# Value weights transposed by DMA on the way in, and newly searched instruction orders, in a recurrent-memory transformer on one core

## The chip, the cores and the metric

The kernel runs on one core of one Trainium2 chip. A core has a matrix engine (TensorE, "PE" in the profile, with its weight loads as "PEld"), three engines for elementwise work (VectorE "DVE", ScalarE "ACT", GpSimd "POOL"), a queue engine (SyncE, "SP") and 16 DMA engines. The metric is the device time of one execution in microseconds (us); less is better. Kernels are compared by the median of their runs.

## What is computed

Two rounds of a recurrent-memory attention layer and a gated MLP, each behind a layer norm and with a residual, on 2048 tokens of width 448:

```python
def _A_ref(x, mem0, Wq, Wk, Wv, Wo, seg_len):      # 16 heads of 256, 8 memory rows, segments of 32
    ...
    for s in range(n_seg):                          # 64 segments, one after the other
        xs = x[:, s * seg_len:(s + 1) * seg_len, :].copy()
        h = jnp.concatenate([mem, xs], axis=1)
        q = jnp.einsum('btd,dhe->bhte', h, Wq)
        k = jnp.einsum('btd,dhe->bhte', h, Wk)
        v = jnp.einsum('btd,dhe->bhte', h, Wv)
        scores = jnp.einsum('bhqe,bhke->bhqk', q, k) * scale
        scores = jnp.where(mask[None, None], scores, -1000000000.0)
        p = _softmax(scores, axis=-1)
        o = jnp.einsum('bhqk,bhke->bhqe', p, v)
        o = jnp.einsum('bhte,hed->btd', o, Wo)
        mem = o[:, :M, :].copy()
        outs.append(o[:, M:, :])
    return jnp.concatenate(outs, axis=1)

def _B_ref(x, W_gate, W_up, W_down):
    gate = jnp.einsum('bsd,df->bsf', x, W_gate)
    up = jnp.einsum('bsd,df->bsf', x, W_up)
    gate = gate * (lambda x, dt: x.astype(dt))(gate > 0, gate.dtype)
    h = gate * up
    return jnp.einsum('bsf,fd->bsd', h, W_down)

x = x + _A_ref(_layernorm(x, axis=-1), A_mem0, A_Wq, A_Wk, A_Wv, A_Wo, A_seg_len)
x = x + _B_ref(_layernorm(x, axis=-1), B_W_gate, B_W_up, B_W_down)
```

The last two lines run twice, with the same weights. All tensors are bf16. The memory rows of a segment come out of the segment before it, so each attention layer is a chain of 64 steps.

## The kernel before

**Folded weights.** Queries and keys are never formed. Per head the kernel builds A = Wq Wk^T (448 x 448) and B = Wv Wo (448 x 448) once and works with these: scores are h A h^T, and the output is the sum over heads of (p h) B. `weights()` does this in the start-up. A product over the head's 256 dims needs that dim on the partitions. Wo lies so in DRAM; Wq, Wk and Wv have their 448 input dims first, so they are loaded as they are into staging slots (`Wst`) and transposed.

For Wv this runs per pair of heads, `p` = 0 to 7. `load` (line 1146) brings 384 of the 448 rows of the pair's 512 columns into slot `sv`; two small DMAs (line 1149) bring the other 64 rows, the "tail"; one DMA (line 1150) brings the pair's Wo into `Wos[so]`. `transposes` (lines 1071 to 1093) makes, per head, seven 128 x 128 transposes on PE into one PSUM bank (six on line 1084, one on line 1085) and two evictions on ACT or DVE into `WT` (lines 1088 and 1091, recorded under the helper's lines 273 and 276). `product` (lines 1095 to 1106) then makes two matmuls of 448 columns (line 1102) from `WT` and `Wos`, and one eviction into `Bsb`: three products per head and one for both tails. The five Wv slots lie in `glu` (12 to 14), where the MLP weights go later, and in `Ug` (15, 16); the profile shows these names. Pairs 5 to 7 use slots 12 to 14 again.

**The two layers run side by side.** `chain` does one step of the recurrence for the first layer and, seven segments behind, one for the second, in the same matmuls: the state's products with A (line 1270), their turn and the scores (1427, 1450), a softmax, the weighted rows (1514, 1518), the product with B (1307), sums on DVE (1324) and the new memory (1349). Around it stands the work that no chain waits for: per tile of 128 tokens the attention of the tokens (`att_group`, lines 1603, 1632, 1514, 1670), norms, and the MLP (`glu_units` line 1692, `glu_down` line 1710).

**Small transposes by DMA.** `turn_dma` (lines 1043 and 1044) issues a transposing DMA on SP. It is used from SBUF to SBUF for the probabilities of the tiles (`Tx<-Px`, 96 times), for the MLP's input (`G<-xn`, 64) and for the probabilities of ridden-along tokens (`PTr<-Pr`, 62).

**A written order.** `_Sched.add` collects 9235 operations with what they read and write. What runs where and when is not left to rules: `ORDER` lists all operations once, each entry being five times the operation's index plus the number of its engine (PE, ACT, DVE, POOL, SP). Each engine runs its own operations in that order and waits at semaphores for what the others must have done. `BANKS` gives the PSUM bank of each allocation in the same order. `FILLS` puts idle matmuls on PE ahead of a given entry: position to (how many, bank, mode); each is a 128 x 128 matmul of a zero tile (line 178). These three tables come from a search outside the kernel.

**DMA semaphores.** DMA n uses semaphore n mod `N_DMA`, and `add` (lines 118 to 123) makes it depend on DMA n - `N_DMA`, which used the semaphore before it. At the end SP waits for the last `N_DMA` entries of its queue that are DMAs (lines 240 to 244).

Of the kernel before, what the change touches and what calls it, by code (L numbers as in the profile page):

```python
# [11 lines left out]
D = 448  # L12
# [38 lines left out]
class _Sched:  # L51
# [5 lines left out]
    N_DMA = 48  # L57
# [222 lines left out]
def bass_interleave_layers__memory_aug_recurrent_mem_tr__glu_gated_reglu__prompt_kernel(  # L280
# [536 lines left out]
class _Kernel:  # L817
# [233 lines left out]
    def weights(self):  # L1051
# [91 lines left out]
        for p in range(NPAIR):  # L1143
# [3 lines left out]
            for hh in range(2):  # L1147
                c = 512 * p + 256 * hh
                self.dma(self.Wst[sv][64 * hh:64 * hh + 64, 3, 0:256], self.Wv_d[0:64, c:c + 256], 32768, w=[("Wt", sv, hh)])
# [688 lines left out]
```

## Time and profile before

| | |
|---|---|
| median of 3 runs | 1563.47 us (1560.84 to 1564.4) |
| the profiled execution | 1558.09 us, of which its span is 1556.3 us |
| granted PE clock | 0.998 |
| instructions | 84947 |
| matmuls | 38530 |
| DMA, mean over the span | 32 GB/s; 16.31 MB of the 49.84 MB move in the first 80 us |
| DMA by SP's queue | 44.15 MB in 113168 packets |

The profile is of one execution. Engine times are busy times; matmuls overlap in the array, so that the durations of PE's instructions add up to more than the time that they take, and a group's price is read from the starts of what follows. "Idle before" is put down to what released the engine last. SP's rows show the issue of a DMA; its landing shows as the end of somebody's wait. The program splits into the start-up until about 75 us, in which all weights are loaded and folded, the two chains with the tiles around them, and an end of some 55 us.

### The profile page before, as it was taken

To read this page: it belongs to the slowest core of one execution; us is meant where nothing else is said; L and a number is where in the kernel's file an instruction comes from. 1 tells how busy PE (TensorE), PEld (TensorE's weight loads), DVE (VectorE), ACT (ScalarE), POOL (GpSimd) and SP (SyncE) were. 2 spreads that over 40 slices of the span, in tenths; PEclk is the share of its full clock that TensorE was granted. 3 is DMA by queue.
4 is the path that set the end of the run, shared out by engine and by line. 5 is a ranking of instruction groups with operands and counts; after the bars stand their busy time and mean duration, and the time that the engine had idled before them with its cause. 6 is when DMAs were issued, how large, how long until landed. Compare 5 with 4: busy or idle time off the path is not lost.

```text
span 1556.3 us, 84947 instructions
## 1 busy us (share of the span) xinstructions
PE 1508.1 (97%) x38530; PEld 1097.1 (70%) x38530; DVE 1127.3 (72%) x3284; ACT 820.6 (53%) x2297; POOL 58.0 (4%) x241
## 2 busy tenths in 40 slices
PE   8999999999999999999999999999999999999998
PEld 6676766667667677767767676777768676777766
DVE  8755678677876777778776778677776777767764
ACT  6754556455555545445555555555555556544442
POOL 1000000000000000000000000000000000000000
PEclk9999999999999999999999999999999999999999
DMA  9422000100100100101001101001001111010101
GB/s 266 145 81 56 12 22 16 18 17 17 23 16 19 27 18 20 19 21 24 19 20 21 29 13 28 17 20 25 20 18 19 26 17 28 19 18 21 20 18 27
DMA packets 114167, 49.84 MB, mean 32 GB/s; under 512 B 82824, under 2 KB 113808, under 8 KB 113808
## 3 DMA queue, kind: packets, MB, share of 16 engines
q1 hardware_dynamic: 113168, 44.15, 12.5%
q8 instruction: 304, 4.98, 1.3%
q14 instruction: 55, 0.45, 0.1%
q10 hardware_dynamic: 640, 0.26, 0.1%
HBM read 21.35 MB, written 1.84 MB: 15 GB/s over the span
## 4 chain that ended last, share of the span: by engine, by line
PE 85%; DVE 7%; DMA 5%; ACT 1%; issue 1%; SPq 1%; ACTq 0%; DVEq 0%; POOL 0%
PE psG L1670 14%; PE psG L1603 14%; PE psG L1692 11%; PE psC L1307 11%; PE psC L1270 7%; PE psG L1710 5%; PE psG L1270 3%; PE psG L1514 3%; PE psG L1102 2%; PE psG L1632 2%; PE psC L1427 2%; DMA Tx<-Px 2%; PE psC L1450 1%; PE psC L1514 1%; PE psG L1427 1%
## 5 line engine op out<-in xcount | busy, mean ns | idle before, releaser
L1670 PE MATMUL psG<-Bsb,YT 128*128 128x448 bf16 x1288 | 277.3, 353 | 0.0
L273 ACT ACTIVATE Ug<-psG 64x128 bf16<-64x128 f32 (+2 forms) x441 | 156.7, 370 | 88.9 <-PE psG L1603 72.2
L1692 PE MATMUL psG<-G,glu 64*128 64x128 bf16 x5838 | 184.6, 216 | 11.5 <-DMA G<-xn 5.0
L1307 PE MATMUL psC<-Bsb,YTm 128*32 128x448 bf16 (+2 forms) x4144 | 187.6, 333 | 0.9 <-issue 0.5
L1692 PEld LDWEIGHTS psG<-G,glu 64*128 64x128 bf16 x5838 | 172.6, 94 | 22.0 <-issue 7.9
L1603 PE MATMUL psG<-HT,A 64*128 64x128 bf16 x3332 | 175.7, 217 | 0.3 <-ACT Bsb L273 0.3
L1670 PEld LDWEIGHTS psG<-Bsb,YT 128*128 128x128 bf16 x1288 | 111.1, 97 | 91.2 <-issue 9.5
L1270 PE MATMUL psG<-A,mT 64*32 64x448 bf16 x4424 | 173.7, 350 | 0.3 <-issue 0.3
L1270 PE MATMUL psC<-A,mT 64*32 64x448 bf16 x3416 | 152.8, 350 | 1.9 <-DVE Tr L1476 1.0
L1603 PE MATMUL psG<-HX,A 64*128 64x128 bf16 x2499 | 150.1, 217 | 0.0
L1307 PEld LDWEIGHTS psC<-Bsb,YTm 128*32 128x32 bf16 x4144 | 102.5, 97 | 65.2 <-DVE YTm L276 2.3
L276 DVE CAST Ug<-psG 64x128 bf16<-64x128 f32 (+2 forms) x265 | 111.1, 429 | 23.1 <-PE psG L1603 18.9
L1697 ACT ACTIVATE hG<-psG 128x512 bf16<-128x512 f32 (+1 forms) x125 | 67.9, 543 | 105.3 <-PE psG L1692 99.1
L1603 PEld LDWEIGHTS psG<-HT,A 64*128 64x128 bf16 x3332 | 116.9, 95 | 8.9 <-issue 5.3
L1324 DVE TENSOR_TENSOR Osum<-psC,Osum 32x448 f32<-32x448 f32 (+2 forms) x120 | 73.2, 610 | 68.7 <-ACT Osum L1322 65.9
L276 DVE CAST YT<-psG 128x448 bf16<-128x448 f32 x148 | 90.2, 618 | 41.3 <-PE psG L1518 40.2
L273 ACT ACTIVATE YT<-psG 128x448 bf16<-128x448 f32 x214 | 107.7, 540 | 20.5 <-PE psG L1518 18.2
L1270 PEld LDWEIGHTS psC<-A,mT 64*32 64x32 bf16 x3416 | 76.5, 92 | 53.8 <-ACT mT L273 3.0
L1270 PEld LDWEIGHTS psG<-A,mT 64*32 64x32 bf16 x4424 | 90.3, 92 | 22.0 <-ACT mT L273 1.9
L1710 PE MATMUL psG<-glu,hG 128*128 128x448 bf16 x434 | 97.5, 353 | 0.2 <-DVE hG L1698 0.2
L1698 DVE TENSOR_TENSOR hG<-hG,psG 128x512 bf16<-128x512 bf16 (+1 forms) x113 | 68.9, 617 | 39.3 <-ACT hG L1697 38.4
L1603 PE MATMUL psG<-l,A 64*128 64x128 bf16 x2919 | 97.2, 216 | 0.0
(294 smaller groups left out, 2910.8 us busy)
## 6 DMA issues: line engine op xcount, KB each, us to landing
Bsb<-in_A_Wq_dram SPq DMA_DIRECT2D x6, 384.0 KB
Bsb<-in_A_Wk_dram SPq DMA_DIRECT2D x6, 384.0 KB
glu<-in_A_Wv_dram SPq DMA_DIRECT2D x6, 384.0 KB
Tsb<-Ohi SPq DMA_DIRECT2D x128, 7.0 KB
X<-in_A_x_dram SPq DMA_DIRECT2D x16, 112.0 KB
glu<-in_A_Wo_dram SPq DMA_DIRECT2D x4, 448.0 KB
out_dram<-X SPq DMA_DIRECT2D x16, 112.0 KB
glu<-in_B_W_gate_dram SPq DMA_DIRECT2D x14, 112.0 KB
```

The costliest lines, as they stand in the source:

```text
L273: return E.activation(out, i, ACT.Copy, scale=1.0 if scale is None else scale)
L276: return E.tensor_copy(out, i)
L1270: i = E.matmul(ub[v].ap()[32 * j:32 * j + 32, 0:D], lhsT=self.mT[rw, b, :], rhs=self.A[rw, b, a0:a0 + D], start=(b == 0), stop=(b == 6), t ...
L1307: x = E.matmul(bo.ap()[32 * j:32 * j + 32, 0:d1 - d0], lhsT=self.YTm[:, q, :], rhs=self.Bsb[:, chunks[q], d0:d1], start=(i == 0), stop=(i ...
L1324: s.add("dve", dv_cost(n), lambda E, e, j=j, a_=a_, part=part: E.tensor_tensor(a_, part(j), a_, ALU.add), r=[bo], w=w, part=(j, 0), **P)
L1514: return E.matmul(ps[:, n * q:n * q + n], lhsT=HR[rows, KM + 128 * q:KM + 128 * q + 128], rhs=PT, start=True, stop=True, tile_position=(b, 0))
L1603: i = E.matmul(ub[v].ap()[:, 128 * n:128 * n + 128], lhsT=self.A[rw, b, a0:a0 + 128], rhs=HT[rw, b, :, 0:SEG] if b < 4 else HX[rw, b - 4, ...
L1670: i = E.matmul(bo.ap()[:, 0:D], lhsT=YT[:, c, :], rhs=self.Bsb[:, 14 * g + c, :], start=(g == 0 and c == 0), stop=(g == 3 and c == 13))
L1692: i_ = E.matmul(two[v].ap()[:, 128 * c:128 * c + 128], lhsT=self.Wgu[rw, b, f0:f0 + 128], rhs=G[rw, b, :], start=(b == 0), stop=(b == 6), ...
L1697: s.add("act", 169 + 0.84 * N, lambda E, e, dst=dst, z=two[0], N=N: E.activation(dst, z.ap()[:, 0:N], ACT.Relu), r=[two[0]], w=[("hG", i, ...
L1698: s.add("dve", dv_cost(N), lambda E, e, z=two[1], N=N, dst=dst: E.tensor_tensor(dst, dst, z.ap()[:, 0:N], ALU.mult), r=[two[1]], w=[("hG", ...
L1710: i_ = E.matmul(bk.ap()[:, 0:D], lhsT=hG[:, c, :], rhs=self.Wd[:, c, :], start=(c == 0), stop=(c == NFC - 1))
```

## The change

Three things.

Wv's loads: instead of a plain load of 384 rows, two tail loads and seven PE transposes per head with two evictions, one transposing DMA per pair brings Wv's 448 x 512 block from DRAM straight into the slot, with the head dims on the partitions (`V`). The products read `V` in the slot in place of `WT`. There are 64 operations less. The transfer's size enters the planner's books as 458,752 bytes.

The tables: `ORDER`, `BANKS` and `FILLS` are new from end to end. 44 filling matmuls in four places become 95 in six. In `ORDER`, the first products of the first Wv pair now come ahead of the last transposes of Wq and Wk.

The semaphores: 96 in place of 48.

```diff
-    N_DMA = 48
+    N_DMA = 96
...
 ORDER = (
     206, 2, 8, 199, 211, 204, 22, 142, 138, 12, 226, 219, 148, 231, 224, 246, 239, 153, 17, 251, 58, 244, 27, 32,
...
-FILLS = {1969: (12, 2, 0), 9083: (15, 0, 0), 9211: (7, 0, 0), 9217: (10, 0, 0)}
+FILLS = {54: (8, 1, 0), 67: (35, 1, 0), 76: (7, 1, 0), 1913: (15, 1, 0), 6778: (15, 2, 0), 8162: (15, 1, 0)}
...
         for p in range(NPAIR):
             sv = 12 + p % 5
             so = p % 5
-            load(self.Wv_d, p, sv)
-            for hh in range(2):
-                c = 512 * p + 256 * hh
-                self.dma(self.Wst[sv][64 * hh:64 * hh + 64, 3, 0:256], self.Wv_d[0:64, c:c + 256], 32768, w=[("Wt", sv, hh)])
+            V = self.Wst[sv].rearrange("p a b -> p (a b)")[:, 0:4 * D].rearrange("p (a b) -> p a b", a=4)
+            self.turn_dma(V, self.Wv_d[:, 512 * p:512 * p + 512], 458752, w=[(z, sv) for z in ("Wst", "Wst3")])
             self.dma(self.Wos[so][:, :, :], self.Wo_d[:, 4 * p:4 * p + 4, :], 458752, w=[("Wos", so)])
-            tv = nw()
-            transposes([(sv, hh) for hh in range(2)], tv, True, self.Wst[sv][:, 3, 0:256], [("Wt", sv, hh) for hh in range(2)])
             tails = []
             for hh in range(2):
-                r = tkeys(tv + hh) + [("Wos", so)]
-                rhs = self.Wos[so][:, 2 * hh:2 * hh + 2, :]
+                r = [("Wst", sv), ("Wos", so)]
+                lhs, rhs = V[:, 2 * hh:2 * hh + 2, :], self.Wos[so][:, 2 * hh:2 * hh + 2, :]
                 for k in range(3):
-                    product(self.Bsb[:, b_idx(k, p, hh), :], [(self.WT[tv + hh], 64 + 128 * k, 128, rhs, 0, r)], [("B", p, hh, k)], 0)
-                tails.append((self.WT[tv + hh], 0, 64, rhs, 64 * hh, r))
+                    product(self.Bsb[:, b_idx(k, p, hh), :], [(lhs, 64 + 128 * k, 128, rhs, 0, r)], [("B", p, hh, k)], 0)
+                tails.append((lhs, 0, 64, rhs, 64 * hh, r))
             product(self.Bsb[:, b_tail(p), :], tails, [("B", p, hh, 3) for hh in range(2)], 3)
```

900 rows, old and new, of tables (BANKS, ORDER) are left out of this document.

## The prediction

> **What bounds the kernel now.** I read the busy shares first, then the same by stage, then what TensorE (PE) waited for, then the start-up instruction by instruction.
>
> ```profile
> PE 1508.1 (97%) x38530; PEld 1097.1 (70%) x38530; DVE 1127.3 (72%) x3284; ACT 820.6 (53%) x2297; POOL 58.0 (4%) x241
> ```
>
> ```profile
> core 0: us, PE busy (x) PEld busy (x) DVE busy (x) ACT busy (x) POOL busy (x), PEclk, DMA share, GB/s
> 0.00:8.40 8.40, 3.25 (x31) 3.05 (x32) 7.05 (x25) 1.28 (x1) 5.85 (x19) 1.00 0.76 214
> 8.40:75.00 66.60, 66.30 (x820) 43.38 (x820) 55.14 (x132) 54.22 (x119) 1.28 (x3) 1.00 0.70 208
> 75.00:300.00 225.00, 211.64 (x5855) 153.16 (x5857) 147.43 (x441) 112.63 (x328) 8.76 (x38) 1.00 0.15 37
> 300.00:1500.00 1200.00, 1176.21 (x30743) 860.11 (x30722) 888.38 (x2612) 633.65 (x1800) 41.89 (x180) 1.00 0.10 21
> 1500.00:1557.00 57.00, 50.73 (x1110) 37.37 (x1106) 29.33 (x77) 18.80 (x50) 0.24 (x1) 0.99 0.12 22
> ```
>
> PE is the bound in every stage, and the granted clock is full. From 8.4 to 75 us, where the weights are transposed and multiplied, PE idles 0.3 us: PE work taken out there shortens the run, unless something else becomes last. The idle time left to win is 5.1 us before 8.4, 13.4 from 75 to 300, 23.8 from 300 to 1500 and 5.6 from there to the span's end at 1556.3. What ended it:
>
> ```profile
> PE psG L1514 <- DMA Tx<-Px: 9.3, 9, 2.2
> PE psG L1084 <- DMA Bsb<-in_A_Wq_dram: 5.1, 2, 4.8
> PE psG L1692 <- DMA G<-xn: 5.0, 4, 1.5
> ...
> PE psC L1514 <- DMA PTr<-Pr: 1.7, 2, 1.0
> ...
> PE psG L1514 <- DMA PTr<-Pr: 1.3, 2, 1.1
> ```
>
> (total us, times, longest). 17.3 us in 17 waits went to the small transposing DMAs Tx, G and PTr; the rest is spread over many single waits on DVE and ACT.
>
> **Part 1: the Wv transposes leave PE.** One group is seven transposes (six on line 1084, one on 1085):
>
> ```profile
> 42.20 0.51 PE L1084 MATMUL psG<-ident,glu 128*128 128x128 bf16 x6
> 42.54 0.22 PE L1085 MATMUL psG<-ident,glu 128*128 128x128 bf16 x1
> ...
> 44.16 1.30 PE L1102 MATMUL psG<-glu 128*128 128x448 bf16 x6
> ...
> 65.07 0.50 PE L1084 MATMUL psG<-ident,glu 128*128 128x128 bf16 x6
> ```
>
> ```profile
> L1085 PE MATMUL psG<-ident,glu x11: 219/219/219, 42.5 to 65.4; 128*128 128x128 bf16 x11
> ...
> L1085 PE MATMUL psG<-ident,Ug x4: 219/219/219, 44.1 to 60.5; 128*128 128x128 bf16 x4
> ...
> L1085 PE MATMUL psC<-ident,glu x1: 219/219/219, 59.7 to 59.7; 128*128 128x128 bf16 x1
> ```
>
> Durations overlap, so the price is from start to start: five groups stand between 42.20 and 44.16, 0.39 us each. 11 + 4 + 1 = 16 groups make **-6.2 us**, all in the stage where PE idles 0.3 of 66.6. Their 32 evictions go too:
>
> ```profile
> L273 ACT ACTIVATE glu<-psG 128x128 bf16<-128x128 bf16 (+1 forms) x12 | 5.3, 503 | 0.5 <-PE psG L1085 0.3
> L273 ACT ACTIVATE glu<-psC 128x768 bf16<-128x768 bf16 (+1 forms) x2 | 1.0, 541 | 0.1
> ```
>
> ```profile
> L276 DVE COPY glu<-psG 128x768 bf16<-128x768 bf16 (+1 forms) x18 | 6.3, 403 | 2.3 <-PE psG L1085 2.1
> ```
>
> About 6.3 us on each of ACT and DVE, which lay beside PE: no gain of their own, but they keep the two from becoming last once PE has 6 us less here.
>
> **Part 2: eight transposing DMAs of 448 KB in place of 24 plain ones.** On SP's queue:
>
> ```profile
> 33.50 2.52 SPq L1049 DMA_DIRECT2D glu<-in_A_Wv_dram  x3
> ```
>
> ```profile
> L1044 SPq DMA_TRANSPOSE G<-xn x64: 1178/1264/2819, 149.4 to 1542.4; - x64
> L1044 SPq DMA_TRANSPOSE PTr<-Pr x62: 1107/1185/2054, 197.5 to 1491.3; - x62
> ```
>
> Three plain issues, some with a wait inside, took up to 2.5 us; one transposing issue takes 1.2 us at 32 KB (PTr) and 1.3 at 96 to 128 KB (G), so 0.03 us per 32 KB and about 1.6 at 448 KB. SP loses nothing. The transfers:
>
> ```profile
> 0.00:26.00 26.00, 20.86 (x252) 15.26 (x253) 22.55 (x67) 15.70 (x36) 6.08 (x20) 1.00 0.99 281
> ...
> 32.00:48.00 16.00, 16.00 (x210) 11.47 (x214) 13.11 (x30) 12.76 (x27) 0.52 (x1) 1.00 1.05 322
> ...
> 406.70:407.50 0.80, 0.80 (x35) 0.77 (x33) 0.43 (x2) 0.72 (x3) 0.00 (x0) 1.00 0.72 164
> 1529.00:1529.60 0.60, 0.60 (x5) 0.30 (x4) 0.22 (x1) 0.35 (x1) 0.00 (x0) 1.00 0.52 109
> ```
>
> (last two numbers: DMA share, GB/s.) The last two windows hold transposing traffic from SBUF to SBUF: 109 GB/s at 0.52 busy, 164 at 0.72, so 210 to 228 GB/s with the engines full, against 322 plain. 458,752 bytes take 1.4 us plain, 2.2 us transposed at full engines, 2.8 at the 164 really reached, 4.2 at 109. No row shows one from DRAM. When would it decide? Wq and Wk are in by 26 us (26 x 281 GB/s = 7.3 MB, their size). The last Wv group stands at 65.07; with 15 groups less ahead of it and part 3's fill, that place comes at about 60. So 34 us are left for eight Wv and eight Wo loads, 4.25 per pair; less 1.4 for Wo that is **2.8 us per transposing load**. I take 2.2, with a row of long bursts behind it: hidden, **0**. Ends: 0, and 8 x (4.2 - 2.8) = +11 us. The same 34 us also cover the other cost: with no copy in WT, staging slots 12 to 14 come free only when the products of pairs 0 to 2 have run, not when their transposes have; in the written order these products end at 38, 42 and 48 of the 62 us of PE work ahead of the first attention product.
>
> The Trainium skill, DMA: Bandwidth & Descriptors, "Why small descriptors are slow (HBM only)", speaks against my SBUF rows: it says that transfers inside SBUF escape a penalty that DRAM ones pay, 27% for pieces of 256 B. By it the 2.2 us would be 2.8 us, an estimate, at the very edge; that is for the second rival below.
>
> **Part 3: fillers.** 44 become 95. Three lots (8, 35, 7) stand among the first transposes, three of 15 late.
>
> ```profile
> L178 PE MATMUL psC<-warm x32: 216/219/219, 1511.2 to 1544.8; 128*128 128x128 bf16 x32
> ```
>
> ```profile
> 1544.44 0.56 PE psC L178 x10
> ```
>
> One costs 56 ns. The 45 late ones replace 44: 0. The 50 early ones are 2.8 us, or fall into PE's idle time before 8.4, where Wq loads were awaited (the 5.1 us above). The order now puts 43 of them before the groups that waited there, but puts the two Wk groups, which ran in that gap, behind: I take **+1.0**, ends -1 and +2.8.
>
> **Part 4: the orders.** An entry of the order is five times an operation plus its engine, so both can be compared. I laid PE's instructions end to end at the trace's own pace, rows like these:
>
> ```profile
> 1491.38 3.23 PE psG L1692 x112
> ...
> 1532.32 5.40 PE psG L1670 x28
> ```
>
> (29 and 193 ns each), and measured for each of the 222 Tx, G and PTr transposes how much PE work is written between the last PE instruction that its data comes from and its first PE consumer. A transfer needs most of this for itself:
>
> ```profile
> 114.00 4.09 DMA Tx<-Px
> ```
>
> 4.1 us from SP's start to landing, plus the softmax or norm ahead of it. Before: 23 have under 7 us, 22 have 7 to 8, 28 have 8 to 9, 149 more. After: 10, 28, 33, 151. So the shortest are halved, the middle hardly moves. In the trace of before 15 of the 17 waits fell among the 73 under 9 us, evenly over the three classes (6.6, 4.1 and 5.2 us). At the same wait per transfer in each class the new order waits 15.6 instead of 17.3: -1.7. The other end: all 17.3 vanish, since a planner that reckons with late landings avoids more than this count sees, such as a wait behind another issue on SP. The same count for waits on ACT and DVE alone shows no shift (the median for the 264 groups of line 1270 is 2.2 us in both). I take **-6**, nearer the counted end.
>
> **Part 5: 96 semaphores.** DMA n no longer waits for n-48 but for n-96.
>
> ```profile
> SPq L1188 <- DMA glu<-in_B_W_down_dram: 3.2, 2, 2.6
> ```
>
> Such waits are few, on SP, with MLP weights behind them that are used tens of us later: 0. At the end SP waits for 96 instead of 48 landings, nearly all long past while the last store travels: 0, at worst +1.
>
> **Sum.** 1558.1 (the profiled execution: span 1556.3 and 1.8 around it) - 6.2 + 0 + 1.0 - 6 + 0 = 1546.9. The median of the runs, 1563.5, stands 5.4 above that execution; the change is expected on it too: **1552 us**.
>
> **The rivals.**
> 1. *The orders pay in full.* Fill hidden, all 17.3 us of waits gone: 1558.1 - 6.2 - 17.3 + 5.4 = 1540. For it: every small DMA was re-planned, and the shortest distances doubled in some places. Against: the middle classes didn't thin out.
> 2. *The weights arrive late (the slower side).* A Wv load from DRAM takes longer than 2.8 us; each us beyond costs 8 us before the first attention product. Against the -11.2 it breaks even at 2.8 + 11.2/8 = 4.2 us, the 109 GB/s of the slower row. At 6 us (76 GB/s): 8 x 3.2 = 25.6 - 11.2 = +14: 1578. For it: no row of a transposing load from DRAM, and engines full for 34 us. Against: 0.72 busy at 164 GB/s with small ones already, and PE's deadline is generous for the first five pairs.
> 3. *The orders give nothing.* The waits move to other places, as a new search balances other things: -6.2 + 1.0 = 1558; with 4 us of new waits on ACT or DVE, or the 50 fillers paid, 1560 to 1563: no change. For it: the count of ACT and DVE distances is the same, the DMA count gives 1.7 only.
>
> **How the numbers follow.** Forecast 0.5, rival 1 0.17, rival 2 0.11, rival 3 0.22. A measurement here can't tell under 0.2%, 3 us. Faster means under 1560.3: the forecast, rival 1 and half of rival 3, 0.78; the other half and a rival 2 near its break-even, 0.12; slower 0.10. The range runs from 1541 to 1562: it leaves out rival 2 and the best half of rival 1.
>
> **What would show it.** Where tile 0's attention began before, the start-up ends:
>
> ```profile
> 74.59 0.56 PE psG L1603 x14
> ```
>
> Part 1: no work of lines 1084 and 1085 on Wv, and this place at 69 us. Part 2: Wv landing within 4 us of its issue, no PE wait on it; a wait on it of over 1 us at 45 to 65 us is rival 2. Part 3: PE idle plus fill before 8.4 us near 6. Part 4: PE's waits on Tx, G and PTr summing to about 11 us; 17 is rival 3, under 3 is rival 1. The forecast fails if the stage from 300 to 1500 us idles more than its 23.8 us.

## The result, and the profile after

The changed kernel takes 1543.82 us (median of 4 runs, 1541.55 to 1548.55) where the kernel before takes 1563.41 beside it: a ratio of 0.9881, with a 95% interval of 0.9852 to 0.991, so 14 to 23 us less. The profiled execution took 1545.7 us, with a span of 1543.7, which is 12.6 under the span before. By stage, with the columns of before:

```profile
core 0: us, PE busy (x) PEld busy (x) DVE busy (x) ACT busy (x) POOL busy (x), PEclk, DMA share, GB/s
0.00:8.40 8.40, 3.34 (x34) 3.35 (x35) 6.21 (x23) 2.26 (x3) 5.88 (x19) 1.00 0.74 207
8.40:75.00 66.60, 64.16 (x759) 41.21 (x759) 49.03 (x112) 49.06 (x105) 1.76 (x5) 0.97 0.90 211
75.00:300.00 225.00, 218.35 (x6038) 157.93 (x6032) 151.11 (x457) 117.14 (x342) 9.45 (x40) 1.00 0.15 36
300.00:1500.00 1200.00, 1182.81 (x30834) 863.61 (x30832) 886.81 (x2577) 640.00 (x1840) 40.48 (x176) 1.00 0.10 21
```

PE's idle time (the length of the stage less its busy time) fell from 13.4 to 6.6 us in 75 to 300 and from 23.8 to 17.2 in 300 to 1500. The start-up went the other way: 2.4 us idle in 8.4 to 75 where there were 0.3, a clock of 0.97 where it was 1.00, and the first attention of tile 0 in the chain of waits stands where it stood, at 74.59 before:

```profile
74.67 0.56 PE psG L1597 x14
```

So the six microseconds of transposes that left PE brought nothing there, and from that place to the end the run is 1469.0 us long instead of 1481.7: all of the gain. PE's own waits (total us, times, longest) say on what:

```profile
PE psG L1100 <- issue: 2.4, 1, 2.4
...
PE psG L1508 <- DMA Tx<-Px: 2.2, 4, 1.0
PE psG L1686 <- DMA G<-xn: 2.0, 2, 1.4
...
PE psG L1508 <- DMA PTr<-Pr: 0.9, 1, 0.9
...
PE psC L1508 <- DMA PTr<-Pr: 0.2, 1, 0.2
```

The waits on the small transposes are 5.3 us, from 17.3. Where the start-up lost its gain is seen on PE and on SP. PE (each row is a run of like instructions, the brackets hold the idle time before):

```profile
38.29 0.54 PE L1100 MATMUL psG<-glu 128*128 128x448 bf16 x2 [2.35 <-issue]
...
39.05 0.83 PE L1082 MATMUL psG<-ident,Bsb 128*128 128x128 bf16 x6
...
39.78 0.85 PE L1082 MATMUL psG<-ident,Bsb 128*128 128x128 bf16 x6
...
43.24 0.50 PE L1082 MATMUL psG<-ident,Bsb 128*128 128x128 bf16 x6
...
43.63 0.50 PE L1082 MATMUL psG<-ident,Bsb 128*128 128x128 bf16 x6
```

SP, each row the issue of DMAs, not their transfer:

```profile
23.57 5.42 SPq L1042 DMA_TRANSPOSE glu<-in_A_Wv_dram  x1
29.04 5.70 SPq L1047 DMA_DIRECT2D HR<-xn  x8
34.79 0.59 SPq L1047 DMA_DIRECT2D glu<-in_A_Wo_dram  x1
35.43 2.17 SPq L1042 DMA_TRANSPOSE glu<-in_A_Wv_dram  x1
...
60.96 1.48 SPq L1042 DMA_TRANSPOSE glu<-in_A_Wv_dram  x1
```

The first transposing issue holds SP for 5.42 us, the eight small `HR<-xn` for 5.70 more, and only then, at 34.79, is the first pair's Wo issued. By the trace's completion records it lands at 38.20 (the first Wv had landed at 31.71), and the product that reads it starts at 38.29. Then four groups of transposes take 0.74 us each (39.05 to 39.78 is the first) instead of the 0.39 of 43.24 to 43.63.

### The profile page after: what moved, and what is told of

It is laid out like the page before. It is cut to its first block, busy times and chain, and to the rows that moved or that the text cites. A ratio compares the mean times of both kernels' runs of the same rounds, so it can differ in the third digit from the quotient of the medians.

```text
span 1543.7 us, 84773 instructions
## 1 busy us (share of the span) xinstructions
PE 1506.9 (98%) x38469; PEld 1094.2 (71%) x38469; DVE 1115.2 (72%) x3225; ACT 823.2 (53%) x2324; POOL 57.8 (4%) x241
## 3 DMA queue, kind: packets, MB, share of 16 engines
q1 hardware_dynamic: 123280, 44.15, 13.3%
## 4 chain that ended last, share of the span: by engine, by line
PE 88%; DVE 6%; DMA 3%; ACT 1%; issue 1%; SPq 1%; POOL 0%; POOLq 0%; DVEq 0%
PE psG L1664 15%; PE psG L1597 14%; PE psG L1686 11%; PE psC L1301 10%; PE psC L1264 9%; PE psG L1704 5%; PE psG L1264 3%; PE psG L1508 3%; PE psG L1100 3%; PE psG L1626 2%; PE psC L1421 2%; PE psG L1301 2%; PE psC L1444 1%; PE psG L1421 1%; PE psC L1508 1%; DMA Tx<-Px 1%
## 5 line engine op out<-in xcount | busy, mean ns | idle before, releaser
L1664 PE MATMUL psG<-Bsb,YT 128*128 128x448 bf16 x1344 | 288.4, 353 | 0.1
L273 ACT ACTIVATE Ug<-psG 64x128 bf16<-64x128 f32 (+2 forms) x412 | 147.8, 376 | 86.0 <-PE psG L1597 71.8
L1664 PEld LDWEIGHTS psG<-Bsb,YT 128*128 128x128 bf16 x1344 | 116.6, 98 | 100.5 <-issue 13.4
L1597 PE MATMUL psG<-HT,A 64*128 64x128 bf16 x3256 | 169.4, 216 | 0.1
L1301 PE MATMUL psC<-Bsb,YTm 128*32 128x448 bf16 (+2 forms) x3696 | 167.3, 333 | 1.7 <-DVE str L1474 1.5
L1264 PE MATMUL psG<-A,mT 64*32 64x448 bf16 x4088 | 163.0, 350 | 0.5 <-issue 0.3
L1301 PEld LDWEIGHTS psC<-Bsb,YTm 128*32 128x32 bf16 x3696 | 91.5, 97 | 58.3 <-ACT Ug L273 1.6
L1318 DVE TENSOR_TENSOR Osum<-psC,Osum 32x448 f32<-32x448 f32 (+1 forms) x106 | 64.9, 612 | 61.4 <-ACT Osum L1316 58.9
L1264 PEld LDWEIGHTS psG<-A,mT 64*32 64x32 bf16 x4088 | 83.0, 92 | 19.9 <-ACT mT L273 2.1
L1597 PEld LDWEIGHTS psG<-HX,A 64*128 64x128 bf16 x2442 | 91.9, 94 | 0.0
```

The costliest lines, as they stand in the source:

```text
L273: return E.activation(out, i, ACT.Copy, scale=1.0 if scale is None else scale)
L1264: i = E.matmul(ub[v].ap()[32 * j:32 * j + 32, 0:D], lhsT=self.mT[rw, b, :], rhs=self.A[rw, b, a0:a0 + D], start=(b == 0), stop=(b == 6), t ...
L1301: x = E.matmul(bo.ap()[32 * j:32 * j + 32, 0:d1 - d0], lhsT=self.YTm[:, q, :], rhs=self.Bsb[:, chunks[q], d0:d1], start=(i == 0), stop=(i ...
L1318: s.add("dve", dv_cost(n), lambda E, e, j=j, a_=a_, part=part: E.tensor_tensor(a_, part(j), a_, ALU.add), r=[bo], w=w, part=(j, 0), **P)
L1597: i = E.matmul(ub[v].ap()[:, 128 * n:128 * n + 128], lhsT=self.A[rw, b, a0:a0 + 128], rhs=HT[rw, b, :, 0:SEG] if b < 4 else HX[rw, b - 4, ...
L1664: i = E.matmul(bo.ap()[:, 0:D], lhsT=YT[:, c, :], rhs=self.Bsb[:, 14 * g + c, :], start=(g == 0 and c == 0), stop=(g == 3 and c == 13))
```

## The experiments

**1. The semaphores alone, on the kernel before.**

```diff
-    N_DMA = 48
+    N_DMA = 96
```

> The kernel before with N_DMA = 96 and nothing else. My theory: the gain past 75 us comes from the new orders, and the semaphores alone do nothing: within 3 us of the kernel before, PE's waits on Tx, G and PTr still about 17 us. Rival: the queue's waits for a free semaphore delayed the small DMAs: then these waits fall to some 5 us and the time by 10 us or more.

Measured: 0.9981 to 1.0031 times the kernel before (1.0006), with 16.1 us of waits on Tx, G and PTr. The semaphores do nothing for the time by themselves, as the theory has it. The new order does need them: with 48, seven of its DMAs stand ahead of the DMA whose semaphore they would reuse.

**2. The new weights path alone**, in the order, with the fillers and the 48 semaphores of before. Three Wv loads and two clears of the Ug tiles stand later than in the order before, since a slot now comes free only behind its products.

```diff
-            load(self.Wv_d, p, sv)
...
+            self.turn_dma(V, self.Wv_d[:, 512 * p:512 * p + 512], 458752, w=[(z, sv) for z in ("Wst", "Wst3")])
```

> The new Wv path in the order, fillers and semaphores of before: the entries of the removed operations are taken out, three loads and two clears of Ug are put later where the slots now come free later. My theory: the gain past 75 us stays away (idle of PE from 75 to 1500 us 35 to 40 us as before), and the start-up gains up to the 6.2 us of the transposes, since nothing of the changed kernel's stall, cold clock and early fill is in this order: 3 to 6 us less than before. Rival: the weights bring most of the gain, 12 us or more. Second rival: the transposing loads are last and the start-up isn't shorter at all, or longer.

Measured: ratio 1.0015 [0.9985, 1.0044], nothing gained, which is the second rival: tile 0's attention starts at 86.23 us instead of 74.59. PE's waits, two of SP's issues, and three pieces of the chain of work that ended last:

```profile
PE psG L1073 <- ACT Bsb L273: 8.9, 3, 7.9
...
PE psG L1073 <- DMA glu<-in_A_Wo_dram: 4.1, 1, 4.1
```

```profile
50.95 4.96 SPq L1020 DMA_DIRECT2D HR<-xn  x8
61.05 1.49 SPq L1015 DMA_TRANSPOSE glu<-in_A_Wv_dram  x1
```

```profile
49.22 3.80 DMA X<-in_A_x_dram
...
53.05 0.63 DVE lnst L1500
...
54.23 0.55 ACT Bsb L273
```

The longest wait, 7.9 us up to 54.83, begins on SP's queue: the tokens `X` go out at 49.22, behind five transposing loads, where the kernel before issues them at 41.43. A layer norm on DVE waits for them until 53.05, and the evictions of the weight products stand behind it. The products come late by that, so between 55.9 and 61.05 SP waits for a slot that comes free behind them; the last Wo is issued only at 70.36, and PE waits 4.1 us for it. So the first part of the change does not pay in this order; the waits on Tx, G and PTr are 14.0 us, near those of before, with 23.7 us idle from 300 to 1490. With experiment 1 this leaves the new tables (the order with its banks, and the late fillers) as the source of the gain after 75 us. A late start is not passed on in full: of the 11.6 us, 6.8 are left at the end of the profiled execution (1563.1 against 1556.3).

**3. No early fillers**, in the changed kernel, run twice.

```diff
-FILLS = {54: (8, 1, 0), 67: (35, 1, 0), 76: (7, 1, 0), 1913: (15, 1, 0), 6778: (15, 2, 0), 8162: (15, 1, 0)}
+FILLS = {1913: (15, 1, 0), 6778: (15, 2, 0), 8162: (15, 1, 0)}
```

> The changed kernel without the 50 filling matmuls of the start (8, 35, 7). My theory: 2.4 us of them stand in time in which PE had work, so attention begins some 2 us earlier than 74.67 and the run is about 2 us shorter than the changed kernel, less what a colder clock costs. Rival: the weight loads, which keep the DMA engines full from 26 to 62 us, set the end of the start-up: no change, PE waits longer for the first Wv product.

> The changed kernel without its 50 early filler matmuls once more, in five rounds beside the others: the start of attention again at 72 to 74 us, no stretch of the start-up below a clock of 0.95, the ratio to the kernel before within 0.982 to 0.989. Theory (the fillers cost 2 to 3 us and buy no clock): the ratio lies below 0.9865. Rival (their cost is hidden in other waits): it is 0.988, as with the fillers.

Measured: ratios 0.9843 [0.9797, 0.9889] and 0.988 [0.9856, 0.9904]; attention starts at 72.86 and 72.28. The second ratio lies on the value of the kernel with fillers, so their price in the time is not resolved by it; in the start-up it is 1.8 and 2.4 us. Most of that is the clock. First the changed kernel, then the first run without early fillers, each with the stall and the stretch behind it (columns as above: length, PE busy and so on, then clock):

```profile
36.00:38.00 2.00, 0.00 (x0) 0.00 (x0) 0.61 (x1) 0.14 (x1) 0.00 (x0) 1.00 0.96 274
39.00:42.00 3.00, 3.00 (x32) 3.00 (x30) 1.17 (x4) 1.96 (x4) 0.00 (x0) 0.51 1.18 305
```

```profile
36.00:38.00 2.00, 0.13 (x2) 0.00 (x0) 0.67 (x2) 0.34 (x1) 0.00 (x0) 1.00 1.02 289
39.00:42.00 3.00, 3.00 (x53) 2.77 (x51) 2.35 (x7) 2.89 (x7) 0.00 (x0) 1.00 1.08 222
```

Both stall at the same product, for 2.35 and 1.97 us (1.55 in the second run). After the longest stall the trace has half the clock for 3.41 us, which costs 1.7; after the two shorter ones it stays at 1.00, and 53 matmuls run where 32 did. The fillers did not keep the clock up there, as they had run long before.

What they do buy lies at the start, and the theory that they "buy no clock" misses it. Two groups of transposes in the changed kernel, then two at the same time without early fillers:

```profile
9.83 0.50 PE L1082 MATMUL psG<-ident,Bsb 128*128 128x128 bf16 x6
...
10.22 0.50 PE L1082 MATMUL psG<-ident,Bsb 128*128 128x128 bf16 x6
```

```profile
9.43 0.84 PE L1082 MATMUL psG<-ident,Bsb 128*128 128x128 bf16 x6
...
10.17 0.84 PE L1082 MATMUL psG<-ident,Bsb 128*128 128x128 bf16 x6
```

That is 0.39 us a group against 0.74, the pace behind the stall above. The first record that the trace has of the granted clock stands at 8.34 us in the changed kernel and at 12.53 and 12.69 in the two runs without early fillers, and up to it the groups go at half pace in all three; the clock column shows 1.00 there because it has no record. So the early fillers bring the full clock some 4 us sooner, worth about 2 us of PE.

**4. The first pair's Wo ahead of the HR DMAs**: one entry of `ORDER`, number 1484, moved from position 227 to 176.

```diff
-771, 1479, 2193, 681
+771, 1479, 1484, 2193, 681
...
-1045, 952, 1484, 1090, 971
+1045, 952, 1090, 971
```

> The changed kernel with the first pair's Wo issued right behind the first Wv instead of behind eight small DMAs. My theory: PE's stall of 2.35 us at 36 us is the wait for this Wo, and the slow transposes after it (0.75 us per group instead of 0.39, granted clock 0.89 in that stage) follow from the stall: both go, attention begins about 4 us earlier, the run is 4 us shorter than the changed kernel. Rival: the stall is the wait for the first transposed Wv; then it stays, within 1 us. Second rival: the stall moves to a later pair because the DMA engines are full.

Measured: ratio 0.9851 [0.9798, 0.9904], attention at 75.65. It is the second rival: the stall left the first pair and came back at the second.

```profile
44.07 8.21 PE L1045 MATMUL psG<-glu 128*128 128x448 bf16 x52 [2.15 <-ACT Bsb L273]
```

```profile
30.50 0.57 SPq L992 DMA_DIRECT2D glu<-in_A_Wo_dram  x1
31.12 6.27 SPq L992 DMA_DIRECT2D HR<-xn  x8
37.43 1.54 SPq L987 DMA_TRANSPOSE glu<-in_A_Wv_dram  x1
```

Wo is in time now, but the second pair's Wv goes out at 37.43, behind the same eight HR DMAs; it lands at 41.40 and its Wo at 43.98, and the products start at 44.07. So the stall is the landing of weights that wait in SP's queue, not the transposing of one pair. The ratio cannot be told from the changed kernel's.

**5. Is it the transposing load or its place on SP?** Two kernels from the changed one. In the first the Wv loads are plain:

```diff
-            self.turn_dma(V, self.Wv_d[:, 512 * p:512 * p + 512], 458752, w=[(z, sv) for z in ("Wst", "Wst3")])
+            self.dma(V, self.Wo_d[:, 4 * p:4 * p + 4, :], 458752, w=[(z, sv) for z in ("Wst", "Wst3")])
```

> The changed kernel, but the eight transposing loads of the value weights are plain loads of 458,752 bytes from the output weights, so the value products are made of the wrong numbers: same places, same queue, same bytes, no transposing in DMA. Theory A (the transposing load is the price, 2.8 us of all engines against 1.4 us for plain bytes and up to 5.4 us of SP while it is issued): the DMA share in 26 to 62 us falls below 0.9, the stall of 2 us ahead of the first value product is gone, the clock stays at 0.95 or more from 32 to 48, and attention starts at 70 to 72 instead of 74.7 us. Theory B (the stall comes from where the loads stand on SP's queue, behind the eight HR DMAs, whatever the load's form): the stall of about 2 us and a start at 74 to 75 us stay. After 300 us nothing changes in either.

In the second the loads still transpose, and the eight HR entries (2204 to 2239) stand behind the Wo of the second pair:

```diff
-862, 735, 2204, 871, 2262
+862, 735, 871, 2262
...
-1001, 1564, 985, 1042
+1001, 1564, 2204, 2209, 2214, 2219, 2224, 2229, 2234, 2239, 985, 1042
```

> The changed kernel with the eight HR DMAs of the start put behind the loads of the first two weight pairs on SP's queue; fillers kept. Theory (the first pairs wait in SP's queue behind the eight HR DMAs, 5.7 us, and not for the transposing itself): no stall ahead of the first value product, clock 0.95 or more from 36 to 48, attention starts at 71.5 to 73 us and the time falls by 2 to 3 us against the changed kernel. Rival (the engines are full, so what the weights gain the HR tiles lose): a stall of 2 us or more stands at a reader of HR or at a later pair, and the start of attention stays within 1 us of 74.7.

Measured: `wv_plain` 0.9882 [0.9853, 0.9911], attention at 70.67; `hr_late` 0.9886 [0.9861, 0.9911], attention at 72.10. Neither has a stall ahead of the products, and the clock stays at 1.00 in both. SP's issues of `wv_plain` and of `hr_late`:

```profile
23.06 0.59 SPq L1047 DMA_DIRECT2D glu<-in_A_Wo_dram  x1
23.70 5.93 SPq L1047 DMA_DIRECT2D HR<-xn  x8
29.67 3.00 SPq L1047 DMA_DIRECT2D glu<-in_A_Wo_dram  x4
```

```profile
23.40 6.07 SPq L987 DMA_TRANSPOSE glu<-in_A_Wv_dram  x1
29.51 0.57 SPq L992 DMA_DIRECT2D glu<-in_A_Wo_dram  x1
30.12 2.63 SPq L987 DMA_TRANSPOSE glu<-in_A_Wv_dram  x1
```

In the start-up `wv_plain` fits theory A and `hr_late` its own theory; both hold for a part. Either cure removes the stall: a first issue of 0.59 us where the transposing one holds SP for 5.4 to 6.1, or the HR DMAs out of the way, which fill tiles that PE first reads at 74.2 us. So the stall needs both, a first load that comes late (the plain one shortens its issue and its transfer together) and 5.7 us of HR DMAs behind it. Why the plain load's start-up is 1.4 us shorter than that of `hr_late` is open. Of the 2.6 and 4.0 us that the start-up gained, the ratios show nothing: they agree with the changed kernel's within their intervals of 0.3%. In the profiled execution of `wv_plain` the 4.0 us are lost again behind that place (1473.1 us from there to the end, 1469.0 in the changed kernel).

What holds the transposing issue is, by the times in these traces, the load ahead of it in the queue. Of the eight in the changed kernel, seven end 0.2 to 0.8 us before that load lands (the first at 28.99, the last Wk load lands at 29.73), and the eighth takes 1.48 us. In `hr_late` and `wo_first` the first one ends 0.85 and 0.78 us before the last Wk load lands. The plain load in the first one's place took 0.59 with the Wk loads still in flight until 29.29.

**6. Both: HR late and no early fillers.** The edits of 3 and of `hr_late`.

> The same, and without the 50 early filler matmuls as well. Theory (stall and fillers each cost their own 2 to 3 us of the start-up): attention starts at 69 to 71 us, against 72.9 with the fillers alone left out, and the time is 3.5 to 6 us less than that of the changed kernel, 1538 to 1541. Rival (the fillers are needed once the stall is gone, or the stall only moves): attention at 72.5 us or later, and the time that of the kernel without fillers (1541) or above.

Measured: 1538.62 us, ratio 0.9866 [0.9842, 0.989], attention at 71.97. By the ratio that is 2.3 us less than the changed kernel, not apart from it or from `hr_late` and under the theory's 3.5; that 1538.62 lies in its span is owed to a kernel before that took 1559.94 beside it. The start of attention fits neither: 0.1 us ahead of `hr_late`. So with the stall gone the fillers cost next to nothing. They are 2.8 us of PE work at the full clock, but without them the first clock record comes at 14.61 us instead of 10.17, and a wait shows that the filled kernel lacks:

```profile
PE psG L1027 <- DMA Bsb<-in_A_Wq_dram: 1.8, 1, 1.8
```

**7. The old order with its late readers moved back.** In the kernel before, PE stood for DMA at 22 transposed tiles in two profiled executions. At 17 of them the readers were moved. At one of these places:

```diff
-3970
...
-3805
...
-3976
...
-3812
...
-3981
...
-3817
...
+3805, 3812, 3817, 3970, 3976, 3981
```

> The kernel before, with its own weights path, its fillers and its 48 semaphores; only the written order is edited. In the two profiled executions of this order TensorE stands at 22 transposed tiles for DMA (17.4 us in the kernel before). For 17 of the 22 the instructions that wait are moved behind as much independent TensorE work as the wait was long, and 1 us more; 5 places, with 5.2 us of the 17.4, are left as they were. Theory (the waits are fixed by the order, and an order that puts the readers later takes them off the time): the waits on Tx, G and PTr fall from 17.3 to 5 to 7 us and the time by 8 to 12 us, to 1552 to 1556 where the kernel before takes 1564. Rival (the readers are late for reasons that the order doesn't set, or what follows them stands in their place): the waits turn up at other tiles, their sum stays at 13 us or more, and the time falls by 0 to 4 us.

Measured: 1599.09 us, ratio 1.0258 [1.0217, 1.0299], 40 us slower. The waits did go, as the theory has it; these are all that is left of them:

```profile
PE psG L1666 <- DMA G<-xn: 2.5, 3, 1.1
...
PE psG L1488 <- DMA PTr<-Pr: 2.0, 1, 2.0
```

(and a third group of 0.4 us.) But PE's waits on DVE and ACT, added up over the list, rose from 17 to 48 us, above all on the tiles' evictions (`Ug`, `YT`) and on the recurrence's rows (`YTm`): PE's idle time grew by 25 us. The other 13 us of the span are PE's own, some 8 of them by the clock (0.993 from 0.998), as here:

```profile
528.00:531.00 3.00, 0.93 (x30) 0.66 (x28) 2.06 (x5) 1.78 (x5) 0.00 (x0) 1.00 0.21 45
531.00:538.00 7.00, 6.28 (x114) 5.25 (x111) 1.32 (x2) 1.14 (x2) 0.00 (x0) 0.53 0.10 20
```

Theory and rival both fell in their numbers. The waits are set by the order, but these 17 moves cost more than they took off: what followed the readers stood in their place, as the rival's second half has it, and by far more than it reckoned.

**8. Early tiles without a new order.** The question left was what the new order gained. In both kernels the 222 small transposes were made plain copies of the same bytes, so that both leave out the turning of these tiles:

```diff
-        self.turn_dma(PT.rearrange("p (g q) -> p g q", g=2), P.rearrange("p g k -> p (g k)"), 65536, r=[("Px", si)], w=[k_("Tx")])
+        self.plain(PT, P.rearrange("p g k -> p (g k)"), 65536, r=[("Px", si)], w=[k_("Tx")])
```

> The kernel before with its 222 small transposing DMAs (Tx, G, PTr) made plain copies of the same bytes between the same tiles, so the attention weights and the MLP's input are used untransposed; order, banks, fillers, semaphores and the weights path are those of before. SP's issue of one falls from 1.2 us or more to about 0.6, and the tile lands 1 to 2 us sooner. Theory (the waits on these tiles come straight off the time, and they are what the new order gained): the waits on Tx, G and PTr fall from 17.3 us to 4 or less, no other wait grows by more than 3 us in sum, and the time falls by 9 to 16 us, to 1548 to 1554 where the kernel before takes 1564, so that before's order with early tiles is about as fast after 300 us as the new order with transposes. Rival (an engine's evictions stand behind the tiles, or the waits move): the waits on those tiles go, others take their place, and the time falls by less than 5 us.

> The same edit in the changed kernel (its eight transposing loads of the value weights stay). Theory: only 5.3 us of waits on Tx, G and PTr are left to take away, so the time falls by 2 to 5 us against the changed kernel, and the lead of 19 to 20 us that it has over the kernel before shrinks to 4 to 10 us against plain_before: what is left of the lead is not in the landing of these tiles. Rival (the new order gained in something else, and landing is not what it was about): the lead over plain_before stays at 15 us or more.

Measured: 1531.17 and 1531.46 us, both 0.9835 [0.9812, 0.9858] of the kernel before. What the edit did to one kind of issue (duration in ns: least, median, most), in the kernel before and in `plain_before`:

```profile
L1044 SPq DMA_TRANSPOSE Tx<-Px x96: 1168/1239/2478, 114.0 to 1527.9; - x96
```

```profile
L1047 SPq DMA_DIRECT2D Tx<-Px x96: 464/517/1590, 113.9 to 1498.6; - x96
```

From SP's start to landing a Tx tile then took 1.9 us in the median instead of 3.1. All the waits on these tiles that are left in `plain_before`, and its stage from 300 to 1500 us:

```profile
PE psG L1517 <- DMA Tx<-Px: 1.2, 3, 0.7
...
PE psG L1517 <- DMA PTr<-Pr: 0.8, 1, 0.8
```

```profile
300.00:1500.00 1200.00, 1192.53 (x31263) 874.09 (x31259) 904.35 (x2665) 645.27 (x1832) 42.14 (x181) 1.00 0.08 21
```

and the same stage of `plain_after`, with 1.3 us of waits on such tiles:

```profile
300.00:1500.00 1200.00, 1191.62 (x31135) 872.88 (x31133) 897.33 (x2612) 647.23 (x1859) 40.99 (x177) 1.00 0.08 21
```

With early tiles the old order is as fast as the new one, within the intervals of 0.23% (3.6 us) on each: 7.5 and 8.4 us idle in this stage, where it was 23.8 and 17.2. So the lead of 19 us hung on these tiles: the old order lost more to their late landing than the new one does. The theory named the place and undersized the price: by the ratios the kernel before gained 26 us and the changed one 7, and of the 4 to 10 us of lead that it expected to stay, none is seen. The edit does two things at once, though: the tile lands sooner, and SP is free 0.7 us sooner for whatever stands behind. Which of the two counts for how much is not shown. 15.3 us of waits on tiles went, and the span fell by 28.6 (1556.3 to 1527.7): 23.0 of idle time and 5.6 of PE's busy time, which the clock (0.998 to 1.000) explains by some 3 us. The rest of the idle time, 7.6 us by the added-up list, was waits on DVE, ACT and others, which went with them.

## Why the prediction was right, and where its steps failed

The forecast was 1552, in a range of 1541 to 1562, and 1543.82 was measured. In the profiled execution the sum gave 1546.9 and 1545.7 was measured: a match by luck, of two errors that cancelled. Up to tile 0's attention the forecast took off 5.2 us and the run none; behind it the forecast took off 6 and the run 12.7.

- **Part 1, -6.2 us: right on PE, not in the time.** The Wv transposes are gone, and `wv_plain` shows about their worth at that place: 74.59 - 6.2 + 2.8 of fillers is 71.2, and its attention starts at 70.67. The changed kernel starts it at 74.67 instead of the 69 that I named, as parts 2 and 3 gave the gain back.
- **Part 2, 0: failed.** The step that failed is "one transposing issue takes ... about 1.6 at 448 KB. SP loses nothing." Unblocked it takes 1.48, but the first, behind Wk loads that are still in flight, takes 5.42, and I had not followed which DMAs stand behind it: the HR ones and the first Wo. That is 2.35 us of stall and 1.7 us of slow clock. "Wq and Wk are in by 26 us" was a misreading that hid it: it took all bytes of that stretch for theirs, and the last Wk load lands at 28.99 in the kernel before and at 29.73 in the changed one. The transfer itself was nearly right. At full engines Wo loads of the changed kernel land 3.84 us apart (41.64 to 57.01, four steps), one for each pair, and plain loads of 448 KB in `wv_plain` land 1.34 us apart (33.90 to 44.61, eight steps), so a transposing load is some 2.5 us: between the 2.2 I took and the 2.8 that would have decided. The other mark, landing within 4 us of the issue, held for one of eight (60.96 to 64.88); the first took 8.1, the others 5.0 to 6.7, queued behind each other at no cost. The estimate of 2.8 us that I worked out by the Trainium skill (DMA: Bandwidth & Descriptors, "Why small descriptors are slow (HBM only)") is a little above what these landings give (taken as 3 of 11 cycles, as the page counts, its 27% would make it 3.0). Its rule is not seen here: in the packet records of the changed kernel, packets of 256 B took 18 ns in the median in these loads and 18 in the small tiles from SBUF to SBUF.
- **Part 3, +1.0: within its ends, and not of one size.** 1.8 and 2.4 us in the changed kernel, where the stall with fillers is followed by the slow clock and the shorter ones without are not; 0.1 where the HR DMAs are late (72.10 against 71.97). "One costs 56 ns" holds at the full clock alone: the first eight take 0.81 us (5.14 to 5.95). That the fillers bring the full clock sooner was no term of the sum.
- **Part 4, -6: mis-sized by half.** The waits fell by 12.0 (17.3 to 5.3), the idle time from 75 to 1500 us by 13.3, and the run behind tile 0's attention by 12.7. What failed is "At the same wait per transfer in each class the new order waits 15.6": the class counts PE work between writer and reader, and in the new order transfers with the same count waited a third as long. From SP's start to landing they are no faster (2.9 us in the mean, after 300 us, against 3.0 before), so the gain shows in where the readers stand: those that start under 0.3 us behind their tile's landing fell from 60 to 33 (of 214 and 216 that the trace lets match). The row of 4.1 us from issue to landing was among the slowest; the median for Tx is 3.1. Experiment 8 ties the lead to these tiles, within its intervals. What rule the search followed is not known from any run.
- **Part 5, 0: right**, by experiment 1.
- **The 5.4 us carried from the profiled execution to the median** was wrong as well: the kernel after was profiled 1.9 above its median, the kernel before 5.4 below its own. This is why the median moved by 19.6 us where the profiled executions differ by 12.4.

Of the rivals, the first (orders pay in full) comes nearest behind the start-up, 17.3 us off against 12.7 measured, but its 1540 lies near by the same luck, as it counts the 6.2 us of the transposes too; the second is what the start-up did, through SP's queue and at 4 us in place of 8 to 25; the third fell with the result itself, where the waits are 5.3 us and not 17. The forecast's breaking condition, over 23.8 us idle from 300 to 1500, was far off at 17.2.

No version tried that computes the same beats the changed kernel for certain. The one without early fillers (0.9843 and 0.988) and the one with HR late as well (0.9866) are at or below its 0.9881, inside the intervals.

## What to carry to other kernels

Before costing a long DMA at its transfer alone, read the queue: how long its issue can hold the queue's engine while earlier loads are in flight, which DMAs stand behind it, and who reads those; four microseconds of the start-up were lost here to a Wo load that nobody had changed. In this kernel, whose PE is 97% busy, late small tiles cost more than the waits that carry their name (28.6 us of span for 15.3 of waits), but moving 17 of their readers by hand in a written order made it 40 us slower: shorten what makes the tiles late, or search the whole order again. And test such a cause by making the tiles early in both kernels: if the difference goes, it hung on them.

## What the runs showed of the hardware

- **A stall of some 2 us can halve the clock behind it, and not its length alone decides.** After 2.35 us without a matmul, and after 2.15 in `wo_first`, the clock was half for 3.41 us; after 1.97 and 1.55 us (the two runs without early fillers) it was not. In the clock records of these thirteen traces the half clock comes in stretches of 3.41 us, or two of them, that lie on a grid of that length. Between the first clock record and the end of the run, each of the 14 grid stretches in which PE idled for 1.94 us or more was followed by one at half clock, and 8 of the 30 with 1.35 to 1.93 us. Of the stall of 1.97 us, 1.67 lay in one stretch. In `plain_after` a gap of 1.27 us, in a stretch with 1.35 us idle, was enough (length, PE busy and so on, then the clock, as above):

```profile
1114.42:1117.83 3.41, 2.06 (x67) 1.70 (x62) 2.04 (x9) 1.32 (x4) 0.00 (x0) 1.00 0.02 5
1117.83:1121.24 3.41, 3.41 (x62) 2.58 (x58) 2.74 (x9) 2.07 (x7) 0.00 (x0) 0.50 0.02 5
```

  The Trainium skill (TensorE: Matmul & The Clock Gate, "HAM oscillation — how this bites in real kernels") warns of gaps above about 3.4 us; these runs show shorter ones doing it.
- **A transposing load from DRAM costs about 2.5 us for 448 KB, a plain one 1.34**, with the DMA engines full (busy shares of 1.08 and 0.95 in these stretches).
- **A transposing issue on SP takes 1.2 us at 64 KB where a plain one takes 0.5, and 1.5 at 448 KB; behind loads in flight it lasts until shortly before they land**, up to 6.6 us (`wo_first`, the first Wv load).
